# An attention kernel fused with a feed-forward layer: four steps of its hand-written order moved, the identity matrix made by GpSimd, 21 places for exponentials and two buffers for activations

## The chip, the cores and the metric

The kernel runs on one core of a Trainium2 chip. The metric is the device time of one execution in microseconds (us), the median of several runs. A core has engines that run side by side, each with its own queue of instructions in a fixed order: TensorE (PE; its weight loads are listed as PEld), VectorE (DVE), ScalarE (ACT), GpSimd (POOL) and SyncE (SP). DMAs are issued from the queues of SP, ACT and POOL; the data is moved by 16 DMA engines. An engine waits at an instruction until the semaphores that it names have come; everything behind it on the same queue waits too.

## What is computed

Inputs are `q`, `k`, `v` of shape (8, 8, 576, 64) (8 batches, 8 heads, 576 positions, head size 64), a table of 32 position buckets by 8 heads, and a feed-forward layer: `w_in` (512 x 2048), `w_out` (2048 x 512), `alpha` (2048).

```python
scores = q @ k.T / 8 + bias_table[bucket(|i - j|)]     # per batch and head
attn   = exp(scores - max) / sum(exp(scores - max))
x      = (attn @ v), heads side by side                # (8 * 576 = 4608, 512)
h      = x @ w_in
g      = h + sin(alpha * h) ** 2 / alpha
out    = g @ w_out                                     # (4608, 512), float32
```

## The kernel before, in words

The work is cut into tasks with short names, made by `_graph` (L46 on), and the order in which they are emitted is written out by hand in the string `ORDER` (L343 on). Each word is a task, with a PSUM bank or an engine behind the slash. `_planned` (L309) goes through it word by word and moves nothing. So each engine's queue is the sequence of that engine's words in `ORDER`, and two words of different engines may change places in the text without any effect on a queue. Semaphore waits are put in by the framework from the places that instructions read and write.

The names that matter here (t is a batch, p a pair of heads, b a block of 512 rows of x):

- `r..`, `f..`: the first loads of k and q (SP and ACT, float32, into the place of the later `toep`) and their casts. `id` loads the 128 x 128 identity (L553, from ACT's queue). `ms` are memsets on DVE.
- `ntpk`: load of a pair of heads of k (k = 0) or q (k = 1) for batches 0 to 2 by POOL, with a cast to float16, 144 KB of destination (L581); `ttpk` turns it on PE with the identity (L703) and `ctpk` copies it to `kT` or `qT`. For later batches `gtk` stages the cast data in DRAM (L608) and `ktk` loads it turned, by a DMA transpose from SP (L614).
- `vtc` and `yta`: loads of v for keys 0 to 511 (four chunks c, L587, 128 KB) and for the last 64 keys (`vt`, two halves, L593, 32 KB), by POOL. There are two buffers, so batch t waits for the attention of batch t - 2.
- `jp`: eight loads that spread the exponentials of the bias into a Toeplitz form (`toep`, L662), four of them from POOL's queue; `mp`: copies on POOL (L668).
- `Ttpwh`, `Xtcq`, `Xtcr`, `St`: scores on PE (L766, L749, L725 or L720). `E...` takes the exponential on ACT (L774) into an exp tile, `B...` multiplies by the bias on DVE.
- `Atpw` and `Lt`: attention times v on PE (L805, L810, L821), which reads exp tiles, `vt` and `vs`. `Ntpw` and `NLt` divide by the sums on DVE (L842, L843).
- `Ytp`: turns the 512 first rows of a batch's x for a pair of heads into `xT`, by a DMA transpose from SP (L850); `YLt`: the last 64 rows of each batch, two DMA transposes (L861). For batch 0 PE does both (`P`, L868 and L877).
- `Ib.f`: h for block b and 128 of the 2048 columns (PE, L887, reads `xT` and `w_in`); `Z` the sine on ACT (L893), `Q` the square (ACT L898 or DVE L900), `G` the sum on DVE (L905) into the block's buffer `g16`. `Otau.i`: the product with `w_out` (PE, L915), `W` its copy out of PSUM, `D` the store.

Attention of later batches is mixed with the feed-forward blocks of earlier rows. Exp tiles of the `T` tasks rotate through `NU` = 13 places of [128, 1024], those of the `X` tasks through `NX` = 4. The g buffer has `NG` = 3 places, each [128, 16, 512]. Block b of the feed-forward layer covers rows 512 b to 512 b + 511 of x, batch t the rows 576 t to 576 t + 575; so block 2 needs the rows of `Y20` to `Y23` and of batch 1, and the late rows of batch 2 (`YL2`) belong to block 3.

The DMAs that POOL issues use eight semaphores in turn, so the ninth waits until the first has landed, and so on.

Of the kernel before, what the change touches and what calls it, by code (L numbers as in the profile page):

```python
# [9 lines left out]
F16 = mybir.dt.float16  # L10
# [9 lines left out]
NU, NX, NG = 13, 4, 3  # L20
# [25 lines left out]
def _graph(K):  # L46
# [21 lines left out]
    ident = add("id", "SP ACT", lambda e, b: K.load_ident(e))  # L68
# [192 lines left out]
    for b in range(NBLK):  # L261
# [88 lines left out]
ET0011 n200 X01r/2 BT0010 c121 m0 EX00r X00q/0 BT0201 BT0110 m1 BT0101 EX01r BT0100 X01q/4 wi1  # L350
T0311/6 BX00r EX01q BT0011 A000/3 n210 BT0300 A010/2 EX00q n220 N000 A001/5 m3 BT0211 ET0311
t110/4 N010 m2 t101/3 T0111/0 c110/A N001 T0301/6 n120 ET0111 BX01r T0310/4 c101 n230 A020/2
ET0301 BT0111 wi2 A021/3 N020 T1000/0 ET0310 wi0 S0/7 N021 t130/6 y11 t231/2 ET1000 BT0301 T1001/4
BX00q A011/3 BT0311 wi3 ES0 c231 c130/A X10r/0 y10 ET1001 A030/7 BT0310 N011 v12 P00/6 BS0 EX10r
P02/2 A031/3 N030 v11 BX01q T1011/4 Y02/A N031 t220/7 ET1011 n221 T1100/0 Y00 T1300/2 c220 P01/6
ET1100 P03/5 Y01 t120/4 BT1011 t210/7 ET1300 T1010/0 c120 L0/6 ET1010 Y03 wo0 t230/4 NL0 t200/5
T1311/2 c200 T1301/0 I0.8/6 ET1311 c230 ET1301 S1/5 c210 X11r/2 v10 I0.0/4 BT1000 EX11r BT1100 v13
I0.3/7 ES1 Z0.0 BS1 BT1010 I0.9/5 BT1300 PL0/3 I0.7/2 YL0 n211 Z0.9 Q0.0 I0.1/3 wo1 Z0.3 Q0.9 G0.0
Z0.7 I0.12/1 v21 Q0.3/A G0.9 I0.2/4 wo2 Z0.8 G0.3 Q0.7/A I0.5/5 n201 Q0.8 Z0.2 G0.7 I0.14/7 Z0.1
Q0.2 Q0.1/A G0.8 I0.10/2 Z0.12 wo3 G0.2 I0.13/6 Q0.12/A BX10r g31 G0.1 Z0.10 I0.4/4 BT1001 Z0.14  # L360
G0.12 A100/3 Q0.10/A Q0.14 I0.11/1 Z0.5 G0.10 g30 Z0.4 G0.14 I0.6/0 Q0.4/A BX11r Z0.11 N100
I0.15/7 G0.4 Q0.5/A y20 O0.0/3 Z0.6 G0.5 O1.0/2 g40 Q0.6/A O0.2 O0.4 Z0.15 G0.6 T1101/4 Z0.13 O1.2
Q0.11 ET1101 Q0.15 O0.6 G0.11 v22 A101/0 BT1301 O0.8 G0.15 A130/1 N101 O1.4 N130 Y10 O1.6 Q0.13
X11q/4 T1111/0 G0.13 t211/7 v20 ET1111 O1.8 c211 O0.10 y21 EX11q BT1111 T1200/0 O1.10 BT1311
ET1200 t201/7 t221/6 T1110/4 c221 T1201/0 ET1110 O1.12 BT1200 O1.14 ET1201 c201 O0.12 T1310/4 v23
W1 X10q/6 ET1310 T1210/0 BT1101 O0.14 BT1110 BX11q A110/2 BT1201 EX10q W0 A111/5 BT1310 D0 ET1210
N110 A120/4 N111 T1211/6 T2100/2 o2 T2110/0 ET1211 Y11 O3.0/5 BT1210 BX10q O3.2 ET2100 BT1211 O3.4
# [12 lines left out]
A221/2 BS2 BT2311 O4.0/3 EX20q N221 O4.2 BT3300 T3301/0 ET3011 T3000/4 Y22 A201/2 BX21q ET3301  # L380
A230/7 N201 k40 A231/6 ET3000 N230 X30r/0 N231 O4.4 EX30r O4.6 BX20q T3001/4 L2/2 ET3001 Y23
T3101/0 NL2 v42 T3211/6 T3100/4 ET3101 O4.8 YL2 v41 O4.10 ET3100 O4.12 y41 O7.0/2 ET3211 BT3100
X31q/0 v31 T3111/4 O7.2 ET3111 Y20 g70 O7.4 O4.14 EX31q X30q/4 W4 T3201/6 O7.6 EX30q BT3011 k41
S3/3 O7.8 g61 BT3000 ET3201 O7.10 BT3110 X31r/0 BX30r BX31q T3200/4 ES3 BT3001 EX31r T3010/6
BT3111 I2.0/3 BT3201 v43 ET3010 A300/1 I2.14/0 ET3200 BT3010 BT3301 N300 I2.5/7 Z2.0 D6 BT3101
BT3200 I2.13/6 BT3211 o4 I2.2/1 Z2.14 A310/5 Q2.14 Z2.2 D4 Q2.0 O7.12 Q2.2/A N310 I2.3/4 Z2.5 G2.0
# [3 lines left out]
G2.15 Z2.8 G2.4 O8.0/3 Z2.12 D5 O8.2 G2.9 A330/0 Q2.8/A Z2.10 X40r/4 Y31 G2.8 A320/1 EX40r N330  # L390
# [3 lines left out]
BX40r O9.8 y50 D8 ET4010 X41r/0 v50 O9.10 T4001/4 EX41r y51 T4211/2 O10.6 YL3 ET4001 v40 O10.8  # L394
O10.10 y40 ET4211 T4100/0 T4101/4 O9.12 v53 ET4100 O9.14 k50 v52 O10.12 W9 ET4101 O10.14 BT4200
T4000/0 T4110/2 T4301/4 ET4000 I3.3/7 ET4110 BT4000 S4/1 I3.15/0 BT4001 k51 ES4 W10 ET4301 A400/3
BT4011 I3.1/6 Z3.15 BT4300 I3.6/2 BX41r N400 BT4101 I3.11/1 Z3.6 Q3.15 I3.5/3 Z3.1 G3.15 Q3.6/A
I3.0/5 Q3.1 Z3.5 G3.1 I3.13/4 Q3.5/A BT4201 G3.6 Z3.0 I3.9/6 G3.5 Z3.13 I3.12/2 Q3.0 Z3.9 G3.0
# [64 lines left out]
class _Ops:  # L463
# [88 lines left out]
    def load_ident(self, eng):  # L552
        self.queue(eng).dma_start(out=self.ident, in_=self.ident_h.ap())  # L553
# [427 lines left out]
```

## Time and profile before

| | |
|---|---|
| median of 3 runs | 380.35 us (380.34 to 381.17) |
| the profiled execution | 381.76 us |
| its span, first to last instruction | 379.9 us |
| mean granted TensorE clock over the span | 0.991 |
| PE busy | 365.4 us, 3769 matmuls |
| ACT busy | 310.5 us |
| DVE busy | 265.3 us |
| POOL busy | 86.0 us |
| DMAs issued by POOL (queue q0) | 18.45 MB |

Times within the trace are counted from the start of the span. A timeline row has the start, the length, the engine (a trailing q marks an instruction that only the queue handles), the line of the kernel, the operation, what it writes and reads, the count of merged instructions and, in brackets, idle time before it and what ended it. In a list of waits stand the total, the number and the longest. A chain row has a start, a length and what the chain spent it on.

### The profile page before, as it was taken

The numbers are of one execution on the slowest core, as the hardware profiler recorded it, in microseconds if no ns is written. First come the engines' busy times: TensorE is split into PE (matmuls) and PEld (weight loads), VectorE is DVE, ScalarE is ACT, GpSimd is POOL, SyncE is SP. The second block draws the span as 40 slices with busy tenths as digits, with TensorE's granted clock in tenths as the row PEclk, the third lists the DMA queues.
The fourth block names the chain that finished last, engine by engine and source line by source line (L and its number), as shares of the span: only waits on it lengthen the run. The fifth ranks groups of instructions, "written<-read, shape, count | busy, mean of one in ns | idle before, by whom it ended". The sixth has DMA issues, their size and how long they took to land.

```text
span 379.9 us, 9143 instructions
## 1 busy us (share of the span) xinstructions
PE 365.4 (96%) x3769; PEld 195.6 (51%) x3769; DVE 265.3 (70%) x613; ACT 310.5 (82%) x417; POOL 86.0 (23%) x104
## 2 busy tenths in 40 slices
PE   4879999999998899999999999999999999999996
PEld 3567445654464455544554555445654564444453
DVE  4789899639975496389754985596729866769412
ACT  5979998999899599899988989999899855686301
POOL 8894682048208000600000050500000000000000
PEclk9989999999999899999999999999999999999999
DMA  9999999999999992890254078980130032020005
GB/s 174 217 170 184 186 193 158 126 201 145 157 131 142 172 100 57 93 155 21 98 129 97 0 83 135 141 69 28 40 89 3 2 83 92 2 83 0 2 29 193
DMA packets 140889, 39.68 MB, mean 104 GB/s; under 512 B 126208, under 2 KB 136304, under 8 KB 140848
## 3 DMA queue, kind: packets, MB, share of 16 engines
q0 software_dynamic: 92864, 18.45, 60.0%
q1 hardware_dynamic: 46272, 18.61, 23.5%
q10 hardware_dynamic: 1712, 2.04, 1.6%
q8 instruction: 29, 0.48, 0.5%
q14 instruction: 12, 0.10, 0.1%
HBM read 36.89 MB, written 15.34 MB: 137 GB/s over the span
## 4 chain that ended last, share of the span: by engine, by line
PE 88%; DMA 6%; ACT 2%; POOL 1%; issue 1%; SPq 1%; DVE 1%; POOLq 0%
PE acc L915 33%; PE acc L887 31%; PE acc L810 8%; PE acc L766 8%; PE acc L805 2%; DMA xT<-xp 2%; DMA v<-in_v_dram 2%; PE acc L821 2%; DMA xT<-in_k_dram 2%; DMA toep<-e_sb 1%; ACT s L893 1%; PE acc L720 1%; PE acc L703 1%; POOL xT L581 1%; PE acc L749 1%
## 5 line engine op out<-in xcount | busy, mean ns | idle before, releaser
L915 PE MATMUL acc<-w_out,g 128*128 128x512 f16 (+1 forms) x592 | 144.3, 374 | 0.0
L887 PE MATMUL acc<-xT,w_in 128*128 128x512 f16 x576 | 135.8, 381 | 2.8 <-DMA xT<-xp 2.2
L774 ACT ACTIVATE u<-acc 128x1024 f16<-128x1024 f32 x128 | 123.7, 1034 | 12.2 <-PE acc L766 11.3
L893 ACT ACTIVATE s<-acc,alphaT 128x512 f16<-128x512 f32 x144 | 91.9, 682 | 23.6 <-PE acc L887 23.0
L905 DVE SCALAR_TENSOR_TENSOR g<-s,inv_a,acc 128x512 f16<-128x512 f16 x144 | 103.2, 742 | 7.3 <-ACT s L898 5.7
L887 PEld LDWEIGHTS <-w_in 128*128 128x128 f16 x576 | 55.3, 98 | 69.2 <-issue 6.5
L915 PEld LDWEIGHTS <-g 128*128 128x128 f16 x592 | 52.7, 98 | 59.0 <-issue 7.3
L797 DVE TENSOR_TENSOR u<-u,toep 128x256 f16<-128x256 f16 (+1 forms) x128 | 58.9, 489 | 19.8 <-ACT u L774 19.5
L587 POOL DMA_DIRECT2D v<-in_v_dram x32 | 30.9, 972 | 145.5 <-PE acc L821 79.0
L810 PE MATMUL acc<-v,u 128*128 128x65 f16 x1024 | 45.4, 196 | 0.5 <-DMA v<-in_v_dram 0.5
L900 DVE TENSOR_TENSOR s<-s 128x512 f16<-128x512 f16 x83 | 34.0, 419 | 17.0 <-ACT s L893 16.7
L810 PEld LDWEIGHTS <-u 128*128 128x128 f16 x1024 | 41.9, 99 | 4.9 <-issue 0.9
L766 PE MATMUL acc<-qT,kT 64*128 64x256 f16 x512 | 42.0, 278 | 1.5 <-DVE kT L653 1.0
L898 ACT ACTIVATE s<-s 128x512 f16<-128x512 f16 x61 | 37.9, 629 | 1.1
L653 DVE COPY outs<-acc 128x512 f32<-128x512 f32 (+1 forms) x24 | 16.2, 675 | 26.7 <-PE acc L915 25.4
L774 ACT ACTIVATE ux<-acc 128x1024 f16<-128x1024 f32 x32 | 32.4, 1035 | 1.8 <-PE acc L720 0.9
L766 PEld LDWEIGHTS <-kT 64*128 64x128 f16 x512 | 20.4, 96 | 22.8 <-issue 18.2
L842 DVE RECIPROCAL rden<-acc 128x4 f32<-128x4 f32 x72 | 12.7, 177 | 25.1 <-PE acc L810 18.7
L805 PE MATMUL acc<-vt,ux 128*128 128x130 f16 x128 | 28.8, 225 | 1.0 <-DMA vt<-in_v_dram 1.0
L843 DVE TENSOR_TENSOR xp<-acc,rden 128x256 f16<-128x256 f32 x64 | 27.2, 424 | 2.3
L651 ACT ACTIVATE outs<-acc 128x512 f32<-128x512 f32 (+1 forms) x13 | 7.6, 582 | 18.6 <-PE acc L915 18.5
L805 PEld LDWEIGHTS <-ux 128*128 128x128 f16 x128 | 12.7, 99 | 8.2 <-issue 2.8
(68 smaller groups left out, 199.2 us busy)
## 6 DMA issues: line engine op xcount, KB each, us to landing
out_dram<-outs SPq DMA_DIRECT2D x30, 256.0 KB, 2.3
v<-in_v_dram POOLq DMA_DIRECT2D x32, 128.0 KB, 6.8
staged_q<-in_q_dram POOLq DMA_DIRECT2D x5, 576.0 KB, 12.4
staged_k<-in_k_dram POOLq DMA_DIRECT2D x5, 576.0 KB, 14.9
w_in<-in_moe_w_in_dram POOLq DMA_DIRECT2D x4, 512.0 KB, 10.5
w_out<-in_moe_w_out_dram POOLq DMA_DIRECT2D x4, 512.0 KB, 10.6
xT<-in_q_dram POOLq DMA_DIRECT2D x11, 144.0 KB, 5.6
xT<-in_k_dram POOLq DMA_DIRECT2D x11, 144.0 KB, 5.9
```

Source lines behind the costliest of these rows:

```text
L587: self.nc.gpsimd.dma_start(out=self.vs[t % 2][:, c, :, 0:D], in_=src)
L766: self.nc.tensor.matmul(out=s[:, o:o + 256], lhsT=self.kT[t % 2][r, p, 128 * c:128 * c + 128], rhs=self.qT[t % 2][r, p, 256 * w:256 * w + ...
L774: self.nc.scalar.activation(out=c["u"], in_=c["s"], func=AF.Exp, scale=0.125)
L797: self.nc.vector.tensor_tensor(out=io, in0=io, in1=m, op=ALU.mult)
L805: nc.tensor.matmul(out=c["av"][:, 130 * j:130 * j + 130], lhsT=cx["u"][:, o:o + 128], rhs=vt[:, p, :], start=True, stop=True, skip_group_c ...
L810: nc.tensor.matmul(out=c["av"][:, 130 * j + 65 * a:130 * j + 65 * a + 65], lhsT=cells[ch // 2]["u"][:, o:o + 128], rhs=vv[:, ch, 2 * p + a ...
L887: self.nc.tensor.matmul(out=c["h"], lhsT=self.w_in[:, j, 128 * f:128 * f + 128], rhs=self.xT[:, j, 512 * b:512 * b + 512], start=(j == 0), ...
L893: self.nc.scalar.activation(out=c["s"], in_=c["h"], func=AF.Sin, scale=self.alphaT[:, f:f + 1])
L898: self.nc.scalar.activation(out=c["s"], in_=c["s"], func=AF.Square)
L900: self.nc.vector.tensor_tensor(out=c["s"], in0=c["s"], in1=c["s"], op=ALU.mult)
L905: self.nc.vector.scalar_tensor_tensor(out=self.g[b][:, f, :], in0=c["s"], scalar=self.inv_a[:, f:f + 1], in1=c["h"], op0=ALU.mult, op1=ALU ...
L915: self.nc.tensor.matmul(out=c["mo"], lhsT=self.g[b][:, f, 128 * (tau % 4):128 * (tau % 4) + 128], rhs=self.w_out[:, f, at], start=(f == 0) ...
```

## The change

The identity is no longer loaded. A memset on DVE (`iz`) clears it, and POOL writes the diagonal with an `affine_select` (`id`), as the second instruction of its queue, behind the load `n011`. ACT's queue loses the DMA at its head.

In `ORDER` many words change their place, but compared queue by queue the sequences of PE, DVE and ACT stay as they were, apart from `iz` and `id`. Four tasks move within a queue:

- POOL: `n110` stood ahead of `v03 v01 y01 v02` and now stands behind them.
- POOL: `v40` and `y40` stood behind `v51 y50 v50 y51` and now stand ahead of them, right behind `v43`.
- SP: `Y20` stood behind `YL2` and now stands ahead of it.

The places: `NU` is 21 and `NG` is 2. Thirteen exp places lie in a tile of their own (`ub`), eight share the memory of a third g buffer (`gb[2]`), which holds g only for the last block; the other blocks alternate in two buffers. The memory used is the same: 13 places and three g buffers.

```diff
-NU, NX, NG = 13, 4, 3
+NU, NX, NG = 21, 4, 2
...
-    ident = add("id", "SP ACT", lambda e, b: K.load_ident(e))
+    clear = add("iz", "DVE", lambda e, b: K.clear_ident())
+    ident = add("id", "POOL", lambda e, b: K.make_ident(), [clear])
...
-                    [q, alpha] + read.get(b - NG, []))
+                    [q, alpha] + (read.get(b - NG, []) if b < NBLK - 1 else []))
...
-id/A r00 ms r10/A r01 n011 r11/A sub n020 cst tab al n021 n100 f00 n031 th00/7 f10/A ch00 n010 f01
+r10/A r00 iz ms r11/A r01 n011 cst sub id tab n020 al n021 f00 n100 f10/A th00/7 n031 th10/6 ch00
...
-t011/7 ET0210 t010/6 j1/G c011 T0211/0 ET0201 T0200/2 j3 c010 at/7 n110 ET0200 av T0101/4 v03
+t011/7 ET0210 j1/G t010/6 c011 T0211/0 ET0201 T0200/2 c010 j3 at/7 v03 ET0200 av T0101/4 v01
+t100/6 ET0101 t031/7 c100 t030/3 y01 t131/2 ET0211 c031 T0100/4 v02 c030 ET0100 n110 c131 T0300/0
...
-T3101/0 NL2 v42 T3211/6 T3100/4 ET3101 O4.8 YL2 v41 O4.10 ET3100 O4.12 y41 O7.0/2 ET3211 BT3100
-X31q/0 v31 T3111/4 O7.2 ET3111 Y20 g70 O7.4 O4.14 EX31q X30q/4 W4 T3201/6 O7.6 EX30q BT3011 k41
+T3111/4 O7.2 ET3111 g70 O7.4 Y20 O4.14 EX31q X30q/4 W4 T3201/6 O7.6 EX30q BT3011 S3/3 g61 O7.8
+BT3000 ET3201 O7.10 BT3110 X31r/0 BX30r BX31q YL2 ES3 T3200/4 BT3001 EX31r BT3111 T3010/6 BT3201
+v43 ET3010 v40 ET3200 BT3010 BT3301 y40 k41 I2.0/3 A300/1 Z2.0 I2.14/0 N300 BT3101 BT3200 BT3211
...
+        self.ub = sgl.tile([128, NU - 8, 1024], F16, name="ub")
+        self.gb = [sgl.tile([128, NF, DM], F16, name=f"gb{i}") for i in range(3)]
...
+    def clear_ident(self):
+        self.nc.vector.memset(self.ident, 0.0)
+
+    def make_ident(self):
+        self.nc.gpsimd.affine_select(out=self.ident, in_=self.ident, compare_op=ALU.not_equal,
+                                     fill=1.0, base=0, pattern=[[-1, 128]],
+                                     channel_multiplier=1)
...
-        c["u"] = self.tp.tile([128, 1024], F16, name=ring, tag=ring,
-                              bufs=NU if ring == "u" else NX)
+        if ring == "u":
+            i = self.nu % NU
+            self.nu += 1
+            c["u"] = (self.ub[:, i, :] if i < NU - 8 else
+                      self.gb[2].rearrange("p f n -> p (f n)")[:, 1024 * (i - NU + 8):1024 * (i - NU + 9)])
+        else:
+            c["u"] = self.tp.tile([128, 1024], F16, name=ring, tag=ring, bufs=NX)
...
-            self.g[b] = self.tp.tile([128, NF, DM], F16, name="g16", tag="g16", bufs=NG)
+            self.g[b] = self.gb[2 if b == NBLK - 1 else b % 2]
```

More of the change, by code (lines that the diff above doesn't have):

```diff
@@ L350 @@
[L350 to L355, printed above, removed]
@@ L386 @@
-BT3200 I2.13/6 BT3211 o4 I2.2/1 Z2.14 A310/5 Q2.14 Z2.2 D4 Q2.0 O7.12 Q2.2/A N310 I2.3/4 Z2.5 G2.0
+r10/A r00 iz ms r11/A r01 n011 cst sub id tab n020 al n021 f00 n100 f10/A th00/7 n031 th10/6 ch00
+f01 n010 ch10 th01/7 y00 T0000/0 ch01/A v00 T0001/2 ET0000 n131 f11 bu/7 ET0001 t020/6 n030 be
+th11/5 bs c020/A t021/4 n121 ch11 bm/7 c021/A n111 T0010/0 bc T0210/2 ET0010 j0 j2/G T0201/4
+t011/7 ET0210 j1/G t010/6 c011 T0211/0 ET0201 T0200/2 c010 j3 at/7 v03 ET0200 av T0101/4 v01
+t100/6 ET0101 t031/7 c100 t030/3 y01 t131/2 ET0211 c031 T0100/4 v02 c030 ET0100 n110 c131 T0300/0
@@ new lines @@
+n101 X00r/6 BT0210 ET0300 BT0200 n231 BT0000 T0110/2 n130 BT0001 t111/5 ET0110 n200 T0011/0 c111
+m0 t121/4 BT0010 ET0011 m1 X01r/2 c121 EX00r wi1 X00q/0 BT0201 BT0110 X01q/4 BT0101 EX01r n210
+T0311/6 BT0100 n220 BX00r EX01q BT0011 A000/3 m3 BT0300 EX00q A010/2 m2 N000 A001/5 BT0211 ET0311
+n120 t110/4 N010 t101/3 n230 T0111/0 c110/A N001 T0301/6 wi2 ET0111 BX01r T0310/4 c101 A020/2 wi0
+ET0301 BT0111 A021/3 y11 N020 ET0310 T1000/0 S0/7 N021 wi3 t130/6 ET1000 t231/2 BT0301 T1001/4
+BX00q y10 BT0311 A011/3 ES0 c231 c130/A v12 X10r/0 ET1001 BT0310 A030/7 N011 v11 BS0 EX10r P00/6
@@ new lines @@
+G0.12 A100/3 Q0.10/A Q0.14 Z0.5 I0.11/1 g30 G0.10 Z0.4 G0.14 I0.6/0 Q0.4/A BX11r Z0.11 N100
+I0.15/7 G0.4 Q0.5/A y20 O0.0/3 Z0.6 G0.5 g40 O1.0/2 Q0.6/A O0.2 Z0.15 O0.4 G0.6 T1101/4 Z0.13 O1.2
+Q0.11 ET1101 Q0.15 O0.6 v22 G0.11 A101/0 BT1301 O0.8 G0.15 A130/1 N101 O1.4 N130 Y10 O1.6 Q0.13
+X11q/4 T1111/0 G0.13 t211/7 ET1111 v20 O1.8 c211 O0.10 EX11q y21 BT1111 T1200/0 O1.10 BT1311
+ET1200 t201/7 t221/6 T1110/4 c221 T1201/0 O1.12 ET1110 BT1200 O1.14 ET1201 c201 O0.12 T1310/4 W1
+X10q/6 ET1310 v23 T1210/0 BT1101 O0.14 BT1110 BX11q A110/2 BT1201 EX10q W0 A111/5 BT1310 D0 ET1210
@@ new lines @@
+ET2301 O5.12 O6.14 D2 A200/5 ET3110 BT2301 O5.14 N200 W6/A T3300/0 T3011/6 W5 X20q/4 ET3300 YL1
+A221/2 BS2 BT2311 EX20q O4.0/3 N221 O4.2 BT3300 T3301/0 ET3011 T3000/4 A201/2 BX21q ET3301 A230/7
+N201 Y22 A231/6 ET3000 N230 X30r/0 N231 O4.4 EX30r O4.6 BX20q k40 T3001/4 L2/2 ET3001 T3101/0 NL2
+v42 T3211/6 T3100/4 ET3101 O4.8 v41 O4.10 Y23 ET3100 O4.12 y41 O7.0/2 ET3211 BT3100 X31q/0 v31
+T3111/4 O7.2 ET3111 g70 O7.4 Y20 O4.14 EX31q X30q/4 W4 T3201/6 O7.6 EX30q BT3011 S3/3 g61 O7.8
+BT3000 ET3201 O7.10 BT3110 X31r/0 BX30r BX31q YL2 ES3 T3200/4 BT3001 EX31r BT3111 T3010/6 BT3201
@@ L393 @@
 BT3310 T4201/4 Y32 O8.14 ET4300 A331/2 W8 ET4201 L3/1 N331 T4011/4 Y33 NL3 v51 T4010/2 O9.6 ET4011
[L394 to L398, printed above, removed]
@@ L434 @@
+EX60q O21.12 BT6310 T7011/4 T7100/6 O21.14 ET7100 YL5 A630/1 W21 A631/0 ET7011 N630 X70r/6 N631
+O22.0/2 EX70r T7101/4 BT7100 Y62 T7110/0 O22.2 BX60q ET7110 L6/7 Y63 ET7101 X70q/0 NL6 O22.4 EX70q
+O20.8 D21 T7301/4 T7000/6 T7201/0 D19 O20.10 ET7000 O20.12 ET7301 O22.6 YL6 I6.5/7 ET7201 I6.8/6
 Z6.5 I6.12/5 I6.13/4 Z6.8 Q6.5 I6.9/1 Q6.8/A G6.5 I6.10/0 BT7101 Z6.9 G6.8 Q6.9/A O22.8 BX70q
@@ L490, in __init__ @@
         self.cst_h = nc.inline_tensor(cst, "cst")
-        self.ident_h = nc.inline_tensor(np.eye(128, dtype=np.float16), "eye")
         self.kT = [sgl.tile([128, NP, S], F16, name=f"kT{i}") for i in range(2)]
```

124 lines of the change are left out of this document (56 added, 68 removed).

## The prediction

> **What bounds the kernel now.** I read the page first (busy shares, chain), then TensorE's waits, then the chain in order of time.
>
> ```profile
> span 379.9 us, 9143 instructions
> PE 365.4 (96%) x3769; PEld 195.6 (51%) x3769; DVE 265.3 (70%) x613; ACT 310.5 (82%) x417; POOL 86.0 (23%) x104
> PE 88%; DMA 6%; ACT 2%; POOL 1%; issue 1%; SPq 1%; DVE 1%; POOLq 0%
> ```
>
> TensorE (PE) is busy for 96% of the span and holds 88% of the chain. No part of the change touches a matmul, so all that it can win is PE's idle 14.5 us (379.9 - 365.4) and whatever makes matmuls longer. Who ends the idle time:
>
> ```profile
> PE acc L688 <- DVE xT L653: 3.9, 1, 3.9
> PE acc L887 <- DMA xT<-xp: 2.2, 1, 2.2
> PE acc L805 <- DMA vt<-in_v_dram: 1.0, 1, 1.0
> ...
> PE acc L810 <- DMA v<-in_v_dram: 0.5, 1, 0.5
> ```
>
> The 3.9 is the start, before the first load has come; three others are DMAs, and two of the moves concern just those: `n110` stands ahead of the value loads on GpSimd's (POOL's) queue, `YL2` ahead of `Y20` on SyncE's (SP's). What the stalls cost beyond their own length is in the table by stretches, cut at the edges of the granted clock's steps (columns: PE busy, weight loads, DVE, ACT, POOL, granted clock, DMA):
>
> ```profile
> 12.44:15.85 3.41, 2.41 (x63) 1.56 (x59) 3.06 (x7) 3.41 (x5) 3.22 (x5) 1.00 1.17 289
> ...
> 19.26:22.67 3.41, 1.41 (x42) 0.92 (x42) 3.41 (x9) 3.41 (x5) 3.24 (x8) 1.00 1.43 176
> 22.67:26.09 3.42, 3.42 (x61) 3.33 (x62) 2.55 (x7) 1.26 (x2) 3.25 (x7) 0.50 1.14 158
> ...
> 121.66:125.07 3.41, 1.25 (x12) 0.53 (x11) 1.83 (x7) 3.39 (x6) 2.16 (x2) 1.00 1.35 111
> 125.07:128.49 3.42, 3.42 (x25) 1.99 (x24) 1.16 (x4) 1.81 (x2) 0.00 (x0) 0.50 1.75 129
> ```
>
> Twice the granted clock is 0.50 for 3.41 us, each time right after a stretch of that length in which PE was busy for only 1.41 or 1.25 us; after 2.41 (12.44 to 15.85) it stayed at 1.00. Each half-clock stretch does 1.71 us of work in 3.41, so it loses up to 1.71 us more. So the two stalls are worth their length plus the clock: that is what I add up.
>
> **Identity on GpSimd.** The DMA of the identity leaves the head of ACT's queue:
>
> ```profile
> 0.74 0.37 ACTq L553 DMA_DIRECT2D ident<-eye  x1
> 1.14 0.98 ACTq L543 DMA_DIRECT2D toep<-in_q_dram  x2
> ...
> 7.63 0.51 PEld L703 LDWEIGHTS <-xT 96*64 96x64 f16 x12 [0.21 <-DMA xT<-in_k_dram]
> ```
>
> The first query load can be issued 0.40 us earlier (1.14 - 0.74), but the gain ends at 7.63, where PE waits for the key load `n020`; and the new select stands right before `n020` on POOL. The memset that it waits for goes first on DVE, and POOL issues `n011` meanwhile; behind the select wait all of POOL's loads. Its time isn't in the trace. The nearest rows:
>
> ```profile
> L608 POOL DMA_DIRECT2D staged_q<-in_q_dram x5 | 12.7, 2549 | 1.0 <-issue 1.0
> ...
> L668 POOL COPY mt<-toep 64x192 f16<-64x192 f16 x8 | 3.1, 388 | 0.3
> ...
> L965 POOL MEMSET const-float32-0.0<- 128x1 f32 x1 | 0.1, 98 | 0.2 <-issue 0.2
> ```
>
> It is an elementwise pass over 128 columns like the copy over 192, so I take 0.4 us; the ends are 0.1 (a memset) and 2.5 (POOL's longest group). PE needs the identity only after its first wait of 3.9, and the select stands second on POOL's queue, so PE won't wait for it. Some 0.1 of the 0.4 is hidden in POOL's own waits: cost 0.3 us (0 to 2.4) on all of the start.
>
> **`n110` behind `v02`.** POOL's queue around it:
>
> ```profile
> 10.42 2.17 POOL L662 DMA_DIRECT2D toep<-e_sb  x4 [0.44 <-DMA xT<-in_k_dram]
> 12.63 0.67 POOL L581 DMA_DIRECT2D xT<-in_k_dram  x1
> 13.37 1.78 POOL L587 DMA_DIRECT2D v<-in_v_dram  x2
> 15.13 0.64 POOL L593 DMA_DIRECT2D vt<-in_v_dram  x1
> 16.38 0.89 POOL L587 DMA_DIRECT2D v<-in_v_dram  x1 [0.60 <-DMA toep<-e_sb]
> ```
>
> 12.63 is `n110`, 15.13 `y01`, 16.38 `v02`. POOL's DMAs wait for the landing of the one eight places before: `v02` for the first Toeplitz load. Moved up one place, `v02` waits for `n111`, issued a DMA earlier, so I drop the 0.60. Then `v03` starts at 12.63 and `v02` at 12.63 + (16.38 - 0.60 - 13.37) = 15.04, plus 0.3 for the identity 15.34: 1.04 us earlier. Its landing ends PE's second stall:
>
> ```profile
> 16.38 6.17 DMA v<-in_v_dram
> ```
>
> With the same 6.17 us it lands at 21.51 instead of 22.55, and `y01`, 0.74 - 0.3 earlier, no longer comes last. PE resumes 1.04 earlier, is busy for about 2.4 of the stretch 19.26 to 22.67, and I expect the clock to hold: + 1.71. `n110` then takes the slot at 16.38 and lands near 22.5, as `v02` did; on PE its transposes stand behind `A000`, `A010` and `A001`, 54 matmuls of which all but the first three wait for `v02`. The 2.75 us are more than the next engine has to give:
>
> ```profile
> ACT kT L651 <- PE acc L703: 2.4, 1, 2.4
> ACT u L774 <- PE acc L766: 11.3, 26, 1.1
> ```
>
> ACT runs without a break into that 2.4 us wait, so it can move by 2.4 - 0.3 = 2.1. And the loads of `w_in` come no sooner:
>
> ```profile
> 26.39 1.51 POOL L598 DMA_DIRECT2D w_in<-in_moe_w_in_dram  x2
> ...
> 40.38 2.76 PE L887 MATMUL acc<-xT,w_in 128*128 128x512 f16 x12
> ```
>
> ```profile
> w_in<-in_moe_w_in_dram POOLq DMA_DIRECT2D x1, 512.0 KB, 11.4
> ```
>
> The second (issued near 27.1, landing 11.4 us later, 38.5) feeds the matmuls at 40.38, so PE can be at most 1.8 us earlier there. **I take 1.8 us for the start**, the identity's cost included; behind that stage the chain is PE's (88% of it) and carries the gain to the end.
>
> **`Y20` ahead of `YL2`.** SP's queue, and what waits:
>
> ```profile
> 114.38 1.22 SPq L850 DMA_TRANSPOSE xT<-xp  x1
> 115.70 2.46 SPq L861 DMA_TRANSPOSE xT<-xl  x2
> 118.21 1.26 SPq L850 DMA_TRANSPOSE xT<-xp  x1
> ```
>
> ```profile
> 118.21 6.32 DMA xT<-xp
> ```
>
> ```profile
> 121.90 0.61 PE L766 MATMUL acc<-qT,kT 64*128 64x256 f16 x8
> 124.66 1.50 PE L887 MATMUL acc<-xT,w_in 128*128 128x512 f16 x4 [2.16 <-DMA xT<-xp]
> 125.95 0.32 PE L805 MATMUL acc<-vt,ux 128*128 128x130 f16 x1
> ```
>
> Block 2 (rows 1024 to 1535) needs `Y20` to `Y23`, not `YL2` (rows 1664 on). `Y20` goes at 115.7, 2.5 us earlier; even with its 6.32 us it lands by 122.0, before PE is free at 122.5. So the 2.16 go. Late next is the value load `v31`, which `A300` needs from its third matmul on:
>
> ```profile
> 117.58 0.92 POOL L587 DMA_DIRECT2D v<-in_v_dram  x1
> ```
>
> ```profile
> v<-in_v_dram POOLq DMA_DIRECT2D x1, 128.0 KB, 6.8
> ```
>
> It lands at 117.58 + 6.8 = 124.4. `I2.0` takes 0.9 us to 123.4, then PE waits 1.0 and goes on at 124.5, where it now does that work at 126.0: 1.5 us. PE is then idle for 1.0 of the stretch 121.66 to 125.07 and busy for 2.4, which is much nearer to the 2.41 that kept the clock than to the 1.41 that lost it. With the clock kept, the 2.4 us from 126.1 to 128.5 take 1.2: together **2.7 us**. ACT lets it through, it waits for PE here:
>
> ```profile
> 128.83 0.69 ACT L893 ACTIVATE s<-acc,alphaT 128x512 f16<-128x512 f32 x1 [1.93 <-PE acc L887]
> 131.42 0.69 ACT L893 ACTIVATE s<-acc,alphaT 128x512 f16<-128x512 f32 x1 [1.90 <-PE acc L887]
> ```
>
> `YL2` goes 1.3 us later than before; it is block 3 that reads it, a whole block behind.
>
> **No cost, no gain.** `v40` and `y40` go past four loads that wait for their buffers, right behind `v43`: PE's list has one wait for v and one for vt, both at the start, so nothing is won here; what it costs is that 160 KB come earlier into the DMA queue, behind the loads named so far. The 21 places: ACT's waits name only scores (L766 above), never a reader of an exp tile, so 13 were enough. Two `g` buffers: on PE, in both orders, the last `O` of block b-2 stands ahead of the first `I` of block b, so no `G` can wait for its buffer. The cover is PE's own order.
>
> **Sum.** 1.8 + 2.7 = 4.5 us. The profiled execution took 381.76 us, 1.41 above the median of 380.35. Either the profile adds those, or a half-clock stretch that the other runs lack (1.71 at most). By the first the result is 380.35 - 4.5 = 375.9, by the second 377.3; I say **376.8**.
>
> A rule of the Trainium skill speaks against my clock terms. The page "TensorE: Matmul & The Clock Gate", section "HAM oscillation — how this bites in real kernels", wants idle gaps of over about 3.4 us before the clock falls; by it neither stall of mine cost any clock. The rows disagree: 1.04 and 2.16 us were followed by 0.50. By the rule the sum is that of rival 2.
>
> **Rivals.**
> 1. Forecast: both stalls go, the clock holds. 375.2 to 377.8. Chance 0.54.
> 2. The half-clock stretches stay, because idle sums of this size still trip them. Left are 1.04 and 1.5: 2.5 us, 377.8 to 379.2, say 378.4. For it: the 2.4 us of both stretches are no more than the least that a row shows to be enough. 0.16.
> 3. The start gives nothing: the select takes 1 to 2.5 us, or the loads land by bandwidth and not by issue. 2.7 us remain: 377.7 to 379.1. Against it: POOL issues back to back before 12.6, so issue is what counts. 0.14.
> 4. Slower. The first select waits for its code, and all POOL loads behind it. Such a fetch would be a DMA, and one of this stage takes 6.17 us (row above): the start loses 6.17 - 1.04 = 5.1, `Y20` gives 2.7: 380.35 + 2.4 = 382.8. It decides from a select of about 4.5 us on, all gains together. No first use of another POOL operation shows such a wait (memset 98 ns). 0.06. A smaller part of "slower" (0.04): the static tiles are guarded as a whole, so that exps wait for readers of other places; slices of one tile loaded and read side by side (xT) speak against it.
>
> The page "GPSIMD Engine Reference", section "2.1 Instruction dispatch", gives about 6 us for the first call of freshly loaded code; no run here shows it.
>
> About 0.3% (1.1 us) can be told from no change. Rivals 1 to 3 lie below 379.2, 0.06 is left for their edges: faster 0.84, same 0.06, slower 0.10. The range reaches from 375.0 (the profile's excess its own, all gains full) to 379.6 (rival 3 with the identity's upper end).
>
> **What would show it.** Right: no wait of L887 for xT<-xp; clock 1.00 throughout; the select under 0.5 us; the waits of L805 and L810 together about 0.9 us near 21, and a new one of 1.0 us for v near 123.4. Wrong: a clock of 0.50 in either place (rival 2), the first key load after the select delayed by more than 1 us (3, 4), any ACT wait for L810.

## The result, and the profile after

| | before | after |
|---|---|---|
| median | 380.76 us (380.34 to 381.35, 4 runs) | 377.49 us (377.14 to 377.94, 4 runs) |
| profiled execution | 381.76 us | 377.77 us |
| its span | 379.9 us | 375.5 us |

The ratio is 0.9915, 95% interval 0.989 to 0.9939: faster by 3.2 us (2.3 to 4.2), where 376.8 us was forecast. Of the span's 4.4 us, 4.0 arrive in the time; what lies outside of the span grew by 0.4.

First the page of the changed kernel: span, busy time, and the chain.

```profile
span 375.5 us, 9140 instructions
PE 362.3 (96%) x3769; PEld 193.2 (51%) x3769; DVE 265.1 (71%) x614; ACT 310.6 (83%) x417; POOL 86.8 (23%) x105
PE 87%; DMA 5%; POOL 3%; ACT 2%; issue 1%; DVE 1%; POOLq 0%
```

PE's busy time fell by 3.1 us, from 365.4 to 362.3, with the same 3769 matmuls; the two half-clock stretches, gone here, cost up to 1.71 each. Its idle time fell from 14.5 to 13.2 only. The chain's share of POOL grew from 1% to 3%.

TensorE's waits:

```profile
PE acc L696 <- DVE xT L661: 5.1, 2, 4.6
...
PE acc L774 <- DVE xp L856: 0.6, 1, 0.6
...
PE acc L818 <- ACT ux L787: 0.5, 1, 0.5
PE acc L823 <- DMA v<-in_v_dram: 0.5, 1, 0.5
```

The waits for `xT<-xp` and for `vt` are gone; one for v is left, and it is the new one of block 2. The first wait has grown from 3.9 to 4.6. The table by stretches, at the edges that the page of before was cut at (PE, weight loads, DVE, ACT, POOL, granted clock, DMA):

```profile
19.26:22.67 3.41, 2.42 (x75) 2.09 (x74) 2.79 (x7) 3.41 (x5) 3.03 (x6) 1.00 1.31 175
22.67:26.09 3.42, 2.61 (x58) 1.81 (x54) 3.02 (x10) 3.18 (x5) 3.25 (x8) 1.00 1.00 131
121.66:125.07 3.41, 2.94 (x30) 1.66 (x29) 2.13 (x9) 3.39 (x4) 2.62 (x4) 1.00 1.04 118
125.07:128.49 3.42, 3.42 (x33) 1.89 (x32) 2.63 (x9) 2.65 (x6) 0.00 (x0) 1.00 2.22 174
```

The clock stays at 1.00 in both places. In the second stretch, though, PE is busy for only 2.61 of 3.42 us: the start is not as full as forecast. POOL's queue, in order of time:

```profile
2.19 0.29 POOL L559 TENSOR_SCALAR_AFFINE_SELECT ident<-ident 128x128 f16<-128x128 f16 x1
2.43 0.64 POOL L589 DMA_DIRECT2D xT<-in_k_dram  x1
...
14.55 0.67 POOL L601 DMA_DIRECT2D vt<-in_v_dram  x1
15.17 0.93 POOL L595 DMA_DIRECT2D v<-in_v_dram  x1
16.40 0.66 POOL L589 DMA_DIRECT2D xT<-in_k_dram  x1 [0.29 <-DMA toep<-e_sb]
...
19.52 0.63 POOL L589 DMA_DIRECT2D xT<-in_k_dram  x1 [0.47 <-DMA v<-in_v_dram]
20.14 1.87 POOL L676 COPY mt<-toep 64x192 f16<-64x192 f16 x4
...
24.04 2.00 POOL L676 COPY mt<-toep 64x192 f16<-64x192 f16 x4
```

The select takes 0.29 us; `n020` behind it is issued at 2.43 instead of 2.04. `v02` goes at 15.17 (15.34 was forecast, 16.38 before). But `n200` (19.52) now waits for `v03`, and the mask copies start at 20.14 and 24.04, later than before (19.83 and 23.33). In this execution VectorE waits for them:

```profile
22.05 0.29 DVE L796 TENSOR_TENSOR ux<-ux,mt 128x256 f16<-128x256 f16 x1 [0.62 <-POOL mt L676]
...
26.08 0.29 DVE L796 TENSOR_TENSOR ux<-ux,mt 128x256 f16<-128x256 f16 x1 [0.29 <-POOL mt L676]
```

Counted in PE's order, the 301st matmul starts 2.15 us earlier than before (23.65 for 25.80), the 361st only 0.91 us (27.39 for 28.30), and from there to 119 us the lead stays at 0.9 to 1.1. At block 2 it grows to 4.27, and ends at 4.4. There SP and PE show:

```profile
113.34 2.53 SPq L863 DMA_TRANSPOSE xT<-xp  x2
115.96 2.47 SPq L874 DMA_TRANSPOSE xT<-xl  x2
```

```profile
121.39 1.04 PE L900 MATMUL acc<-xT,w_in 128*128 128x512 f16 x4
122.99 0.37 PE L823 MATMUL acc<-v,ub 128*128 128x65 f16 x7 [0.47 <-DMA v<-in_v_dram]
```

`Y20` goes with `Y23`, ahead of `YL2`; the first matmuls of block 2 wait for nothing, and `v31` makes PE wait 0.47 us, where 1.0 was forecast.

### The profile page after: what moved, and what is told of

The parts are those of the page before. It is cut to its first block, busy times and chain, and to the rows that moved or that the text cites. A ratio compares the mean times of both kernels' runs of the same rounds, so it can differ in the third digit from the quotient of the medians.

```text
span 375.5 us, 9140 instructions
## 1 busy us (share of the span) xinstructions
PE 362.3 (96%) x3769; PEld 193.2 (51%) x3769; DVE 265.1 (71%) x614; ACT 310.6 (83%) x417; POOL 86.8 (23%) x105
## 3 DMA queue, kind: packets, MB, share of 16 engines
HBM read 36.86 MB, written 15.34 MB: 139 GB/s over the span
## 4 chain that ended last, share of the span: by engine, by line
PE 87%; DMA 5%; POOL 3%; ACT 2%; issue 1%; DVE 1%; POOLq 0%
PE acc L928 33%; PE acc L900 31%; PE acc L774 8%; PE acc L823 8%; DMA v<-in_v_dram 3%; PE acc L818 2%; PE acc L834 2%; ACT s L906 1%; DMA xT<-in_q_dram 1%; PE acc L728 1%; POOL xT L589 1%; POOL mt L676 1%; PE acc L711 1%; PE acc L757 1%; ACT s L911 1%
## 5 line engine op out<-in xcount | busy, mean ns | idle before, releaser
L928 PE MATMUL acc<-w_out,gb 128*128 128x512 f16 (+1 forms) x592 | 144.3, 374 | 0.0
L918 DVE SCALAR_TENSOR_TENSOR gb<-s,inv_a,acc 128x512 f16<-128x512 f16 x144 | 103.3, 743 | 7.3 <-ACT s L911 5.7
L787 ACT ACTIVATE ub<-acc 128x1024 f16<-128x1024 f32 x80 | 77.8, 1033 | 8.0 <-PE acc L774 7.5
L928 PEld LDWEIGHTS <-gb 128*128 128x128 f16 x592 | 52.7, 98 | 59.0 <-issue 7.3
L787 ACT ACTIVATE gb<-acc 128x1024 f16<-128x1024 f32 x48 | 46.5, 1030 | 4.8 <-PE acc L774 4.5
L810 DVE TENSOR_TENSOR ub<-ub,toep 128x1024 f16<-128x1024 f16 (+1 forms) x80 | 36.6, 478 | 7.3 <-ACT ub L787 7.1
L823 PE MATMUL acc<-v,ub 128*128 128x65 f16 x640 | 34.9, 193 | 0.6 <-DMA v<-in_v_dram 0.5
L823 PEld LDWEIGHTS <-ub 128*128 128x128 f16 x640 | 30.6, 97 | 4.0 <-issue 1.3
L810 DVE TENSOR_TENSOR gb<-gb,toep 128x1024 f16<-128x1024 f16 (+1 forms) x48 | 23.2, 501 | 11.5 <-ACT gb L787 11.5
L855 DVE RECIPROCAL rden<-acc 128x4 f32<-128x4 f32 x72 | 12.8, 177 | 20.8 <-PE acc L823 14.5
```

The source lines that it names most:

```text
L787: self.nc.scalar.activation(out=c["u"], in_=c["s"], func=AF.Exp, scale=0.125)
L810: self.nc.vector.tensor_tensor(out=io, in0=io, in1=m, op=ALU.mult)
L823: nc.tensor.matmul(out=c["av"][:, 130 * j + 65 * a:130 * j + 65 * a + 65], lhsT=cells[ch // 2]["u"][:, o:o + 128], rhs=vv[:, ch, 2 * p + a ...
L918: self.nc.vector.scalar_tensor_tensor(out=self.g[b][:, f, :], in0=c["s"], scalar=self.inv_a[:, f:f + 1], in1=c["h"], op0=ALU.mult, op1=ALU ...
L928: self.nc.tensor.matmul(out=c["mo"], lhsT=self.g[b][:, f, 128 * (tau % 4):128 * (tau % 4) + 128], rhs=self.w_out[:, f, at], start=(f == 0) ...
```

## The experiments

Theory: the gain is the sum of three ends of waits (`Y20`, `v02`, and the clock that the two stalls cost). Rivals: the start gives nothing that lasts; something in the part costed at nothing counts. Each part was run alone, and the sum, each on one of three chips (a, b and c); the kernel before ran beside them (medians 380.88, 380.70 and 380.82 us).

| kernel | chip | median, us | ratio to before | 95% interval |
|---|---|---|---|---|
| `Y20` alone | a | 377.97 | 0.994 | 0.9914 to 0.9967 |
| `n110` alone | a | 381.24 | 1.0015 | 0.9987 to 1.0042 |
| identity alone | a | 380.32 | 0.9987 | 0.9959 to 1.0016 |
| after, masks early | a | 378.28 | 0.9928 | 0.9903 to 0.9952 |
| the whole change | b | 377.80 | 0.9928 | 0.9904 to 0.9953 |
| start alone (identity and `n110`) | b | 380.37 | 0.999 | 0.9965 to 1.0015 |
| the rest alone | b | 380.11 | 0.9977 | 0.9957 to 0.9997 |
| after, `v31` earlier | b | 376.79 | 0.9901 | 0.988 to 0.9923 |
| after, `v40 y40` put back | c | 378.59 | 0.9928 | 0.9904 to 0.9952 |
| places alone | c | 380.94 | 0.9994 | 0.9969 to 1.0018 |
| identity loaded late | c | 381.55 | 1.0009 | 0.9983 to 1.0035 |
| after, `v31` and `k40` | c | 377.27 | 0.9894 | 0.9868 to 0.9921 |

**`Y20` alone.**

```diff
-SP: k40 Y23 YL2 Y20 k41
+SP: k40 Y23 Y20 YL2 k41
```

> The kernel before with one move: Y20 ahead of YL2 on SP's queue. Theory A (the stall and the clock that it costs both go): the wait of 2.16 us for xT at the first matmuls of block 2 disappears, a wait of 0.4 to 1.0 us for the value load v31 appears in its place, the granted clock stays 1.00 after 125 us while the half-clock stretch after 22.67 us stays; 2.7 to 3.3 us faster than the kernel before. Theory B (the half-clock stretch has another cause than the stall): a stretch of 0.50 after 125 us stays, about 1.5 us faster. Theory C (the order alone does nothing, the gain of the whole change in this place comes from the more places or the other buffers): less than 1 us.

TensorE's waits in this kernel:

```profile
PE acc L689 <- DVE xT L654: 3.8, 1, 3.8
PE acc L704 <- DMA xT<-in_k_dram: 0.9, 1, 0.9
PE acc L811 <- DMA v<-in_v_dram: 0.6, 1, 0.6
```

The 2.2 are gone, 0.6 us for `v31` came. It is 2.3 us faster (1.3 to 3.3): theory A's mechanism, its size by the median below A's 2.7 to 3.3. Theory C falls. Theory B's 1.5 us lies within the interval, but its half-clock stretch does not come: the clock is 1.00 throughout this trace, and 3 of its 12 runs show a lowered clock against 19 of 35 of the kernel beside it. The half-clock stretch after 22.67 us, expected to stay, is not there either.

**`n110` alone, the identity alone, and both.**

```diff
-POOL: n111 j2 j1 n110 v03 v01 y01 v02 n101
+POOL: n111 j2 j1 v03 v01 y01 v02 n110 n101
```

> The kernel before with one move: n110 behind v02 on POOL's queue, the identity still loaded by a DMA. Theory A (POOL's mask copies cap the start, as the trace of the changed kernel suggests): v02 lands about 1.2 us earlier, no wait for v is left at the first attention matmuls, n200 waits for v03's landing, the masks come no earlier than before, and of about 2 us won at 22 us some 1.0 to 1.4 us are left behind 28 us; 1.0 to 1.4 us faster. Theory B (the cap is ACT's wait and the landing of w_in, as predicted; the rest of the loss in the changed kernel was the identity's): 1.8 to 2.1 us faster. In both the clock stays 1.00 at 22.67 and falls to 0.50 at 125.

```diff
-ACT: id r10 r11 cst
+ACT: r10 r11 cst
-DVE: ms
+DVE: iz ms
-POOL: n011 n020
+POOL: n011 id n020
```

> The kernel before with the identity made by GpSimd and nothing moved. Theory A: the select takes 0.3 us and holds POOL's later loads back by 0.4 us; PE's first transposes start 0.7 us later, because the first load of k shares the DMA engines with that of q, but by 8 us only 0.2 to 0.4 us of this are left; the whole is 0.1 to 0.4 us slower than the kernel before. Theory B (the first use of the operation waits for its code): 5 us slower. Theory C (the query load issued 0.4 us earlier counts): 0.3 us faster.

The start alone is both diffs together.

> The kernel before with the two edits of the start (identity by GpSimd, n110 behind v02), Y20 left behind YL2. Theory A (the start gives nothing that lasts): within 0.5 us of the kernel before. Theory B (as the first two profiles suggested, 1.0 us at 28 us): 1.0 us faster. The recorded prediction: 1.8 us faster. In the profile, key load n020 lands before 7.5 us although it is issued 0.4 us later, if its landing hangs on the load of the identity that is gone and not on chance.

Alone, neither can be told from no change, nor can both: 0.4 us faster (0.6 slower to 1.3 faster). The recorded 1.8 us and both theories of `n110` alone (A's 1.0 to 1.4, B's 1.8 to 2.1; 0.5 faster at most) lie outside of these intervals; theory B of the start alone, 1.0, does not. Theory B of the identity, 5 us slower, falls. `n020` lands at 7.2 in the start alone, as expected there.

The traces show why `n110` alone can't be worth what the sum made of it: the wait that it ends is one execution's. Of the six traces with `n110` in its old place, only that of before waits for vt (1.04 us) and v (0.54) near 21 us and has a half-clock stretch behind it; the rest alone waits 0.4 us for v, the other four not at all. In three of these four PE ran at half speed until 20.9 to 25.3 us and came to the place later (last section). In the trace of `Y20` alone, for one, the list above has no wait for `vt`, and the one for v is `v31`'s. The waits of `n110` alone:

```profile
PE acc L689 <- DVE xT L654: 3.8, 1, 3.8
PE acc L888 <- DMA xT<-xp: 2.7, 2, 2.1
...
PE acc L704 <- DMA xT<-in_k_dram: 0.7, 1, 0.7
```

`n020` landed 6.8 us after its issue (5.5 in before), so that PE lost 0.7 us there, and the masks again held VectorE up:

```profile
23.33 0.29 DVE L784 TENSOR_TENSOR ux<-ux,mt 128x256 f16<-128x256 f16 x1 [1.01 <-POOL mt L669]
```

**Masks early.**

```diff
-POOL: n130 n200 m0 m1 wi1 n210 n220 m3 m2 n120
+POOL: n130 m0 m1 m3 m2 n200 wi1 n210 n220 n120
```

> The changed kernel with the four mask copies on POOL together, ahead of n200, wi1, n210 and n220 (m3, m2 and n200 moved; the loads behind come 1.5 to 2 us later). Theory A (the masks are what took the start's gain from 2.1 us at 22 us to 1.0 us at 28 us): the masks end near 23 instead of 26.04, DVE's two waits for them (0.62 and 0.29 us) and PE's wait of 0.60 us at 25.84 go, PE is 0.8 to 1.1 us earlier at 30 us; 0.6 to 1.1 us faster than the changed kernel, if w_in still lands in time. Theory B (ACT, which runs gapless there, or w_in is the cap): PE at most 0.3 us earlier, the time within 0.3 us of the changed kernel. Theory C (the delayed loads n210, n220 or wi1 come late): slower by up to 1 us, with a wait for one of them.

The masks of this kernel on POOL, and what VectorE's second mask and PE met:

```profile
19.36 4.34 POOL L677 COPY mt<-toep 64x192 f16<-64x192 f16 x8
```

```profile
25.66 0.28 DVE L797 TENSOR_TENSOR ux<-ux,mt 128x256 f16<-128x256 f16 x1
```

```profile
32.77 0.45 PE L712 MATMUL acc<-ident,xT 96*64 96x96 f16 x12 [0.43 <-DMA xT<-in_k_dram]
```

VectorE no longer waits for masks, but PE's wait of 0.6 us just before 25.8 stays (0.61 here), and PE's 361st matmul is only 0.38 us earlier than in the profile after (1.29 us earlier than before). A load behind the masks comes late, PE waits 0.43 us for it at 32.77, and the lead is 0.77 at 34 us. The ratio equals that of the whole change. Theory A holds for VectorE's waits alone and fails for PE's and for the time; the late load is one that theory C named, but a slower time can't be told.

The unchanged order shows the same without the move. In the second profile of the whole change (next paragraph), the masks come early by themselves and VectorE does not wait for them:

```profile
19.48 1.51 POOL L676 COPY mt<-toep 64x192 f16<-64x192 f16 x4
...
23.03 1.86 POOL L676 COPY mt<-toep 64x192 f16<-64x192 f16 x4
```

```profile
25.32 0.28 DVE L796 TENSOR_TENSOR ux<-ux,mt 128x256 f16<-128x256 f16 x1
```

PE's 361st matmul is 1.63 us earlier than before there. So late masks come and go between executions, and are not shown to limit the start.

**The whole change beside its parts.**

> The whole change again, beside its parts. Theory A (all of the gain is Y20's, the start gives nothing that lasts): 2.3 to 3.0 us faster than the kernel before, as Y20 alone was. Theory B (the start's part is worth about 1 us, as the two first profiles suggested): 3.3 to 4.0 us faster.

2.7 us faster (1.8 to 3.7), 3.2 in the first measurement. Between theories A and B it does not decide.

**The rest alone, then its two halves.** The rest is 21 places, two g buffers and

```diff
-POOL: v43 ... v51 y50 v50 y51 v40 y40 v53
+POOL: v43 v40 y40 ... v51 y50 v50 y51 v53
```

> The kernel before with only the rest of the change: 21 places for exp tiles, two g buffers, v40 and y40 ahead of v51 y50 v50 y51. Theory A (no cost, no gain, as predicted): within 0.5 us of the kernel before, no wait of ACT for the attention matmuls and none of DVE for a g buffer. Theory B (the loads v40 and y40 issued 36 us earlier free PE of a small wait near 164 us, or the other places cost something): a difference of 0.3 to 1 us with a change of PE's position between 160 and 170 us.

0.9 us faster (0.1 to 1.6), by the median outside of the 0.5 us of theory A, mine; the interval still reaches into it. Which half is it?

```diff
-NU, NX, NG = 13, 4, 3
+NU, NX, NG = 21, 4, 2
```

> The kernel before with 21 places for exp tiles and two g buffers, nothing moved. Theory A (the places cost and give nothing, the 0.9 us of the run with v40 and y40 moved as well were those loads'): within 0.4 us of the kernel before. Theory B (the places are what gave the 0.9 us): 0.7 to 1.1 us faster.

```diff
-POOL: v43 v40 y40 ... v51 y50 v50 y51 v53
+POOL: v43 ... v51 y50 v50 y51 v40 y40 v53
```

> The changed kernel with v40 and y40 back behind v51 y50 v50 y51. Theory A (the move of v40 and y40 is worth something, because y40 landed only 0.14 us ahead of its use in the profile of before and may be late in other executions): a wait for vt of 0.1 to 1 us at the first attention matmuls of batch 4, near 160 us; 0.3 to 0.9 us slower than the changed kernel. Theory B (no cost, no gain, as predicted): the same time as the changed kernel within 0.3 us.

The places alone: 0.2 us (0.7 slower to 1.2 faster), no change to be told. The loads: in the trace of before, `y40` is issued at 159.31 and lands 5.1 us later, at 164.45; its reader starts at 164.59.

```profile
155.43 0.89 POOL L587 DMA_DIRECT2D v<-in_v_dram  x1 [31.62 <-PE acc L821]
...
159.31 0.69 POOL L593 DMA_DIRECT2D vt<-in_v_dram  x1
```

```profile
164.59 0.22 PE L805 MATMUL acc<-vt,ux 128*128 128x130 f16 x1
```

This looks like slack, and is none, as the same row shows with the old order in "places alone", in "v40 y40 put back" and in "identity loaded late", each from its own trace:

```profile
164.37 0.22 PE L814 MATMUL acc<-vt,ux 128*128 128x130 f16 x1 [0.69 <-DMA vt<-in_v_dram]
```

```profile
161.15 0.22 PE L819 MATMUL acc<-vt,ux 128*128 128x130 f16 x1 [1.38 <-DMA vt<-in_v_dram]
```

```profile
164.52 0.22 PE L806 MATMUL acc<-vt,ux 128*128 128x130 f16 x1 [0.78 <-DMA vt<-in_v_dram]
```

In all three PE starts 0.13 or 0.14 us after `y40` has landed, as in before: there too PE had been released by it. None of the six traces with `v40` and `y40` moved up shows a wait in this place: from the start of the four matmuls ahead of it to this row PE takes 0.86 or 0.87 us in all six. In the eight with the old order it takes 0.86 (`Y20` alone), 1.00 (before), 1.1 (`n110` alone, the identity alone) and 1.7 to 2.4 (the three above and the start alone, where the list puts the wait down to ACT, but `y40` lands 0.13 us ahead of PE's start). That is 0.6 us lost on average of the eight.

Why it varies, the same traces show. POOL issues `y40` 4.1 us after PE has freed the buffers (the end of L821 in the row of 155.43), in all eight, and PE's own work from there to the reader is 9.25 us. So `y40` comes late when it takes more than about 5.0 us to land (an estimate: 9.25 - 4.1 - 0.13), and it took 4.8 to 6.5. POOL's queue moves with PE here, so a lead won earlier does not by itself make `y40` late.

In the times, "put back" cannot be told from the whole change (the two ran on different chips); its trace, with the longest of the waits, carries theory A, and the size in the time stays open between 0 and 0.9 us.

**`v31` and `k40`, the version beyond.** What is late next for block 2 was seen in the profile after, so it was moved as well:

```diff
-POOL: v42 v41 y41 v31 g70 g61 v43
+POOL: v31 v42 v41 y41 g70 g61 v43
```

> The changed kernel with v31 three places earlier on POOL's queue, ahead of v42, v41 and y41. Theory A (v31 is what comes late once Y20 is in time): the wait of 0.2 to 0.6 us for v near 123 us goes and nothing takes its place, 0.2 to 0.6 us faster than the changed kernel. Theory B (v31 waits for a buffer that is freed only near 116 us, or the loads behind it become late): the wait stays or moves to v42 or v41, no gain.

```diff
-SP: k40 Y23 Y20 YL2 k41
+SP: Y23 Y20 k40 YL2 k41
```

> The changed kernel with v31 ahead of v42, v41 and y41 on POOL and k40 behind Y20 on SP. Theory A (Y20 and v31 are the only loads that come late for block 2, and k40, which holds SP for 3.4 us ahead of Y23, has time): no wait for xT or v between 120 and 125 us, Y20 lands 2 us earlier or more, 1.0 to 1.4 us faster than the changed kernel and 0 to 0.4 us faster than with v31 alone. Theory B (k40 behind Y20 is late for batch 4, or Y23 waits for something else and goes no earlier): a new wait for kT between 130 and 150 us, no gain over v31 alone.

With `v31` alone the wait for v goes and one for `xT` comes:

```profile
PE acc L901 <- DMA xT<-xp: 0.7, 1, 0.7
```

Yet it is 3.8 us faster than before (2.9 to 4.6), 1.0 us by the medians faster than the whole change on the same chip: more than the 0.2 to 0.6 expected. The whole change's own trace on that chip lists no wait for v in this place, so the gain is not explained by that wait alone. With `k40` behind, the three loads go in one piece, and there is no wait for v or xT left:

```profile
108.38 5.77 SPq L864 DMA_TRANSPOSE xT<-xp  x3
114.25 3.76 SPq L623 DMA_TRANSPOSE kT<-staged_k  x1
```

4.0 us faster than before (3.0 to 5.0), the best ratio; against `v31` alone it can't be told. Both versions beat the two kernels of this case by their medians, in part on other chips.

**The identity loaded late.**

```diff
-ACT: id r10 r11 cst
+ACT: r10 r11 id cst
```

> The kernel before with the load of the identity behind the two loads of q on ACT's queue. In all runs so far n020 lands at 7.59 to 9.15 us where the identity is loaded, and at 7.07 to 7.45 us where GpSimd makes it, though it is issued 0.4 us later there. Theory A (the earlier loads of q free the DMA engines for n020): q lands by 5.5 us instead of 6.4 and n020 by 7.5. Theory B (the identity's own load stands in n020's way, or the 0.4 us by which n020 is issued earlier bring nothing but contention): n020 lands after 7.5 us. In both PE's first transposes wait for the identity, to about 4.5 to 5 us instead of 3.85, and the time is within 0.6 us of the kernel before.

`n020` landed at 7.8 us with q's loads early: theory A fails. PE waited for the identity longer than expected, to 6.0 us:

```profile
PE acc L689 <- DMA ident<-eye: 6.0, 1, 6.0
```

and the whole was 0.3 us slower (1.3 slower to 0.6 faster): 2.2 us later at PE's first instruction are nearly lost from sight at the end.

## Why the prediction was right, step by step

**The total.** 376.8 was said between two readings of the profile's excess of 1.41 us; the second (half-clock stretches that other runs lack) gave 377.3, and 377.49 came. The runs bear it out: of 81 timed runs of the kernel before, 39 had a mean clock of 0.998 or more, 27 of 0.994 to 0.996, 15 of 0.990 or 0.991. The profiled execution, with 0.991, was one of the 15. I should have taken the second reading. That 376.8 came so near is in part luck: the start's 1.8 us in the sum were too many (0.4 by its own run) and the nothing for the rest too little (0.9), and the two errors make up for one another in part.

**1, identity.** 0.4 us for the select: right (0.29 measured, 0.39 of delay on POOL). "Cost 0.3 us on all of the start": not seen; alone it was 0.5 us faster (0.6 slower to 1.6 faster). `n020`, issued 0.39 us later, landed no later: at 7.45 for 7.59. In all eight traces with the select it landed by 7.45, in the six that load the identity at 7.59 to 9.15. What I had not counted is that k's first load lands later when q's is issued beside it (3.98 us for 3.42), and PE starts 0.71 us later; 0.21 of this are left at 9 us. Rival 4 (a fetch of code) did not occur. The Trainium skill's "GPSIMD Engine Reference", section "2.1 Instruction dispatch", has about 6 us for a first call of freshly loaded code; the first select here took 0.29 us, and POOL waited for nothing ahead of it that the trace shows.

**2, `n110`: the start's 1.8 us.** This term was too large. In the profile after, `v02` went 1.21 us earlier (1.04 said), the clock held, and of the 0.9 us of waits for v and vt forecast near 21 none came. But the two things that the sum priced here, a wait of 1.04 us and a half-clock stretch behind it, were one execution's: none of the five other traces with the old order has that stretch, and the longest of their waits for v or vt there is 0.4 us. Nor does this move keep the clock in the timed runs: with `n110` moved and `Y20` not, 13 of 24 show a lowered clock, as 42 of 81 of the kernel before do. By position the start gives something all the same: in the six other traces with both start edits PE's 1501st matmul starts at 117.5 to 118.9 us, in the profile after at 118.56, in the five with neither at 118.8 to 120.3, about 1.4 us earlier on average. The time of the start alone shows 0.4, at most 1.3. In its trace PE's lead falls by 0.94 at the first matmul that reads `y40`, which took 6.1 us to land there (5.1 in before). Whether that is all of the difference stays open. So rival 3 came nearer than the forecast for this part.

**3, `Y20`: 2.7 us.** 2.3 (1.3 to 3.3) alone. The step holds: the wait goes, `v31` is late next (0.47 for 1.0), the clock stays. The clock's 1.2 us, though, are not there every time. Of the kernel before, 42 of 81 runs show a lowered clock; with `n110` moved and `Y20` not 13 of 24; with `Y20` alone 3 of 12; with both moved, in all such kernels together, 1 of 39 (0.998 and more is counted as full). So the clock's share of the gain is a price times a chance, and it goes with the place of `Y20`; what sets the chance stands in the last section. The Trainium skill's page "TensorE: Matmul & The Clock Gate", section "HAM oscillation — how this bites in real kernels", asks for idle gaps of over about 3.4 us; by it these stalls, of 1 to 2 us each, would never have cost any clock. The 42 of 81 and the 1 of 39 speak against that.

**4, "no cost, no gain".** This step failed. Places and buffers: right, as far as can be told (0.2 us faster, 0.7 slower to 1.2 faster). `v40` and `y40`: "PE's list has one wait for v and one for vt, both at the start, so nothing is won here". The list held what one execution happened to show. PE's start 0.14 us behind a landing was the sign that no slack was left. With the old order `y40` cost PE 0 to 1.5 us from trace to trace, by how long it took to land (4.8 to 6.5 us); moved up, it cost nothing in any of six. How much of this the time shows is open: 0.9 us (0.1 to 1.6) for the rest alone, nothing when it was put back.

The parts alone add up to 2.3 + 0.4 + 0.9 = 3.6 us, the whole gave 3.2 and 2.7, within the intervals. My 4.5 had 1.8 for a part that gave 0.4 by the median and nothing for one that gave 0.9.

## What to carry to other kernels

A list of waits shows one execution: beside each wait look at the loads that land within a few tenths of their use, because those are the waits of other runs. The same holds for a wait that the list names: five other traces had next to nothing of the one that was priced at 1.04 us and the clock. When a stall is removed, follow the queue of each engine that feeds the place, also those that are off the path, and look at a second execution before calling something the next limit: the mask copies that held VectorE up in the first profile after did not in the second. Loads in a queue belong in the order in which their data is needed: swaps of that kind (`Y20`, then `v31`) carried most of what was won here.

## What the runs showed of the hardware

- What lowers the clock in these traces is not the length of a stall but how little PE is busy within one step of the clock. The granted clock changes only on a grid of 3.41 us, which lies differently in each execution. In `n110` alone PE waited 2.08 us for `Y20`, and with the identity loaded late 2.15 us. Cut at each trace's own steps, the first leaves PE busy for 1.93 us, and the clock stays at 1.00; the second leaves 1.50, and 0.50 follows. The third pair is the end of `v31` and `k40`, where 1.56 still keep the clock.

```profile
120.31:123.72 3.41, 1.93 (x18) 0.72 (x13) 2.42 (x8) 3.41 (x6) 3.24 (x3) 1.00 1.58 102
123.72:127.14 3.42, 2.82 (x29) 1.67 (x30) 1.62 (x6) 3.17 (x4) 0.00 (x0) 1.00 1.49 151
```

```profile
120.27:123.69 3.42, 1.50 (x13) 0.54 (x11) 2.40 (x9) 3.42 (x5) 2.80 (x2) 1.00 1.57 102
123.69:127.10 3.41, 3.18 (x24) 1.83 (x25) 0.26 (x2) 2.44 (x3) 0.00 (x0) 0.50 1.68 134
```

```profile
369.96:373.37 3.41, 1.56 (x15) 1.16 (x12) 0.69 (x1) 0.40 (x2) 0.00 (x0) 1.00 0.68 250
373.37:376.78 3.41, 0.00 (x0) 0.00 (x0) 0.00 (x0) 0.00 (x0) 0.00 (x0) 1.00 0.01 2
```

- In all 14 traces of this case, from the first full step of the clock's record on, each step with 1.50 us or less is followed by 0.50 and none with 1.56 or more is. By this a stall of 2.16 us costs the clock in about half of its places on the grid (an estimate: (3.41 - 2.16 + 2 x 0.25) / 3.41 = 0.51, with no other idle time in the step), near the 13 of 24 in which this stall was left and `n110` moved.
- At the start PE runs at half speed until the first entry of the clock's record, though the column of the granted clock reads 1.00 there: the same twelve matmuls take 0.69 us in `Y20` alone and 0.45 in before.

```profile
20.46 0.69 PE L704 MATMUL acc<-ident,xT 96*64 96x96 f16 x12
```

```profile
17.95 0.45 PE L703 MATMUL acc<-ident,xT 96*64 96x96 f16 x12
```

- That first entry stands at 11.2 to 14.5 us in eleven traces and at 20.9 to 25.3 in three (`Y20` alone, the identity alone, the places alone), all with `n110` in its old place; it is at 11.2 to 13.6 in the seven with both start edits. What sets it was not tried.
- Two lowered stretches go with 1.6 to 2.3 us in the time, not with 2 x 1.71: means of 382.04, 381.86 and 382.22 us on the three chips against 379.85, 380.28 and 379.97 at full clock.
- The latency of one and the same load, `n020`, ran from 4.6 to 7.1 us between executions. The identity's load goes with the high values, but neither its order nor the select's delay was separated from it.
- Time outside of the span is a kernel's own: 1.97 to 2.01 us on average for before, 2.14 with the select, 2.24 with the places alone, 2.3 with all. So 0.3 us of the gain never reach the time. The cause was not tried.
